# Decay rows of a gated linear attention: by transposes for the first four chunks, by earlier DMAs for the others, and a range flag summed in the tail

## The chip, the core and the metric

The kernel runs on one core of one Trainium2 chip. Its time is device microseconds (us) of one execution; the median of several runs is compared. The engines are TensorE (PE; its weight loads are shown apart as PEld), VectorE (DVE), ScalarE (ACT), GpSimd (POOL) and SyncE (SP), which here issues all DMAs. PE writes to PSUM, DVE and ACT carry results from there to SBUF.

## What is computed

A gated linear attention over 4 batches, 8 heads, 768 positions and head size 48 makes 3072 tokens of width 384. A gated product with w1, w2, w3, w_out (1024 wide) follows, then a soft mixture of 8 experts with 4 slots each, whose weights come from softmaxes of x @ phi over tokens and over slots:

```python
f = 1.0 / (1.0 + np.exp(-f_logit))
for t in range(S):
    state = f[:, :, t, :, None] * state + np.einsum('bhd,bhe->bhde', k[:, :, t], v[:, :, t])
    y[:, :, t] = np.einsum('bhd,bhde->bhe', q[:, :, t], state)
...
h = ((x @ w1) * (x @ w2)) @ w3
x = h @ w_out
...
logits = x @ phi
```

The weights w1, w2, w3 and w_out come as 64-bit floats, and the kernel decodes them on DVE.

## The kernel before, in words

The tokens are cut into 24 chunks of 128 positions; chunk n is chunk n // 4 of batch n % 4, so chunks 0 to 3 are the first ones of the four batches. In each chunk the recurrence is done as matmuls:

- `att_decay(n)` makes -log f of the forget gates on ACT and DVE (tiles in_f, nlh, nll).
- `att_scale(n)` sums it along positions with two matmuls by a triangle (pl), caps it on DVE (lc), and writes exp(-lc) into `eqp` (ACT, L561) and exp(lc) into lc. `eqp` is one tile, used again by every chunk. POOL makes kp = k * exp(lc), DVE makes qp = q * eqp (L564).
- `att_transpose(n)` transposes qp and kp in PE, four 128x128 pieces each (tq and tk), and ACT copies them out (qT, kT). The last row of eqp is what the whole chunk decays by. It is needed as columns, with the state's rows on partitions; the kernel before gets this by two DMAs (L583, L584), one from eqp into a row of DRAM (dec_d), one back as a column (dec).
- `att_scores(n)` multiplies kT by qT (pa) and DVE masks it (att, two halves). `att_out(n)` adds up the output (py) from the state and from att, takes the running minimum test okt of dec on DVE, and updates the state: pk, then tmp on DVE, then S = tmp * dec on POOL (L646).

Beside that, `w_ld`, `w_dec` and `w_low` load the six pairs of pieces of w1 and w2 (weight pairs 0 to 5), decode them in three DVE steps each (L793, L796, L799), and make the low parts of the weights (two matmuls each by identity and minus identity, pw). `glu_mm` makes the products with w1 and w2 in three passes of high and low parts (pp, L675, nine 512 column matmuls in a group). `j_ld`, `j_dec` do the same decode for w_out and w3.

The order of PE's work is written out by hand (`manual_schedule`); at the start it is att_scale(0), att_transpose(0), w_low(0), att_scores(0), w_low(1), att_out(0), att_scale(1), att_transpose(1), w_low(2), then the first GLU matmuls. The order on the other engines, and that of SP's DMAs, is chosen by a scheduler when the program is built, from when it thinks each can run. Each engine runs its own list in order, so an instruction that waits holds up all behind it.

At the very end of the chunks, `range_flag` and `range_flag2` reduce okt and the checks of the weights to one number `flag`, with one small matmul (pfl) and two DVE steps; when it is 0, a slow general version runs after. Then the tail computes the experts (`layer2`), the slots' outputs (`slot_out`) and the final sum (`combine`), and writes the output.

Of the kernel before, what the change touches and what calls it, by code (L numbers as in the profile page):

```python
# [10 lines left out]
F32 = mybir.dt.float32  # L11
# [9 lines left out]
P = 128  # L21
# [9 lines left out]
def kernel(  # L31
# [15 lines left out]
    nc = tc.nc  # L47
# [6 lines left out]
    NP = H // 2  # L54
# [3 lines left out]
    KD = DM // P  # L58
    KF = FF // P
    XB = 8  # L60
    HF = FF // 512


# [16 lines left out]
    w3_d = dpool.tile([FF, FF], F32, name="w3_d")  # L80
    wo_d = dpool.tile([FF, DM], F32, name="wo_d")
    flag = cst.tile([1, 1], I32, name="flag")
    dec_d = dpool.tile([2, H * DP], F32, name="dec_d")

    def soft_exp(pool, lg, lsum, mx):

# [466 lines left out]
    def att_scale(n):  # L553
        a = at[n]
        i = n % 2
        pl = psum.tile([P, 512], F32, tag="ps", name="pl")
        nc.tensor.matmul(pl[:, 0 : H * D], lhsT=trir, rhs=a["nlh"], start=True, stop=False)
        nc.tensor.matmul(pl[:, 0 : H * D], lhsT=trir, rhs=a["nll"], start=False, stop=True)
        lc = att_p.tile([P, H, D], F32, name="lc")
        nc.vector.tensor_scalar_min(flat(lc), pl[:, 0 : H * D], DECAY_CAP)  # L560
        nc.scalar.activation(out=eqp[:, :, 0:D], in_=lc, func=AF.Exp, scale=-1.0)  # L561
        nc.scalar.activation(out=lc, in_=lc, func=AF.Exp)  # L562
        nc.gpsimd.tensor_mul(kp[i][:, :, 0:D], a["k"], lc)  # L563
        nc.vector.tensor_mul(qp[:, :, 0:D], a["q"], eqp[:, :, 0:D])  # L564

    def att_transpose(n):
        a = at[n]
        i = n % 2
        qf = qp.rearrange("p h d -> p (h d)")
        kf = kp[i].rearrange("p h d -> p (h d)")  # L570
        tq = psum.tile([P, 512], F32, tag="ps", name="tq")
        for p in range(NP):
            nc.tensor.transpose(tq[:, p * P : (p + 1) * P], qf[:, p * P : (p + 1) * P], ident)  # L573
        qT = att_p.tile([P, NP, P], F32, name="qT")
        nc.scalar.copy(qT, tq.rearrange("p (a t) -> p a t", a=NP))
        tk = psum.tile([P, 512], F32, tag="ps", name="tk")
        for p in range(NP):
            nc.tensor.transpose(tk[:, p * P : (p + 1) * P], kf[:, p * P : (p + 1) * P], ident)  # L578
        kT = att_p.tile([P, NP, P], F32, name="kT")
        nc.scalar.copy(kT, tk.rearrange("p (a t) -> p a t", a=NP))  # L580

        dec = att_p.tile([P, NP, 1], F32, name="dec", bufs=2)
        nc.sync.dma_start(out=dec_d[n % 2 : n % 2 + 1], in_=eqp[P - 1 : P].rearrange("o h d -> o (h d)"))  # L583
        nc.sync.dma_start(out=dec.rearrange("p a o -> p (a o)"), in_=dec_d[n % 2].rearrange("(a r) -> r a", r=P))  # L584
        a.update(qT=qT, kT=kT, dec=dec, kf=kf)

    def att_scores(n):
        a = at[n]
# [407 lines left out]
    def range_flag():  # L996

        rok = keep.tile([P, 1], F32, name="rok")
        nc.vector.tensor_reduce(out=rok, in_=okt, axis=AX.X, op=ALU.min)
        cm1 = keep.tile([P, 1], F32, name="cm1")  # L1000
        for cm, lim, red, op in (
            (cmx, HI_MAX * HI_MAX, ALU.max, ALU.is_le),
            (cmn, 0.5, ALU.max, ALU.is_lt),
        ):
            nc.vector.tensor_reduce(out=cm1, in_=cm, axis=AX.X, op=red)
            nc.vector.scalar_tensor_tensor(out=rok, in0=cm1, scalar=lim, in1=rok, op0=op, op1=ALU.mult)
        return rok

    def range_flag2(rok):
        pfl = psum.tile([P, 512], F32, tag="ps", name="pfl")  # L1010
        nc.tensor.matmul(pfl[0:1, 0:1], lhsT=rok, rhs=ones, start=True, stop=True)
        okf = keep.tile([1, 1], F32, name="okf")
        nc.vector.tensor_scalar(out=okf, in0=pfl[0:1, 0:1], scalar1=P - 0.5, scalar2=None, op0=ALU.is_ge)
        nc.vector.tensor_copy(flag, okf)
# [212 lines left out]
    region.close()  # L1227
    while pf:
        pf.pop(0)()
    range_flag2(range_flag())  # L1230

    a, b, n = NCH - 3, NCH - 2, NCH - 1
    assert p == a - 1 and m_next == NCH and nchk[0] == NCK
# [42 lines left out]
    with ExitStack() as st:  # L1276
# [146 lines left out]
        def combine(t, g):  # L1423

            w = (2 - t) * P
            ot = order[used[0] % len(order)][0].tile([P, FF], F32, tag="raw", name="ot")[:, 0 : 4 * w]
            used[0] += 1
            ot = ot.rearrange("p (a f) -> p a f", a=4)
            for i in range(0, 4, 2):
                pf_ = tps.tile([P, 2, 2 * P], F32, tag="ps", name="pf")  # L1430
                for u_ in range(2):
                    nc.tensor.matmul(pf_[:, u_, :], lhsT=cT[:, 4 * g + i + u_, :], rhs=sst[t], start=True, stop=True)
                if i:
                    nc.scalar.copy(ot[:, i : i + 2], pf_[:, :, 2 * P - w : 2 * P])
                else:
                    nc.vector.tensor_copy(ot[:, i : i + 2], pf_[:, :, 2 * P - w : 2 * P])
            nc.sync.dma_start(
                out=out.rearrange("(b c p) f -> c p b f", b=B, p=P)[g, :, :, 2 * t * P : 2 * t * P + w], in_=ot
            )

        cs = range(KF)
        half = (range(KF // 2), range(KF // 2, KF))
        layer2(0, 0, cs)
# [9 lines left out]
        combine(0, 2)  # L1453
        layer2(1, 1, half[1])
        combine(0, 3)
        slot_out(1)
        combine(0, 4)
        combine(0, 5)
# [47 lines left out]
```

## Time and profile before

| | |
|---|---|
| median of 3 runs | 522.74 us (522.02 to 524.37) |
| the profiled execution | 524.82 us, of which 523.1 us are the profile's span |
| PE busy | 469.9 us (90%) |
| DVE, ACT, POOL busy | 261.4, 256.6, 95.6 us |
| mean granted TensorE clock | 0.971 of 2.4 GHz |
| moved by DMA | 85.44 MB, mean 163 GB/s |

Times in the rows are us from the span's start. A row of the timeline gives start, length, engine, line and operation, out<-in, shape, and in brackets how long the engine stood before it and what ended that. PE busy is not PE at its peak. The chain of waits is followed back from the last instruction: each piece is what released the next.

### The profile page before, as it was taken

The page shows a single profiled execution, that of the slowest core. Times are in us where ns is not written, and L with a number is a line of the kernel's source. Part 1 is how long each engine was busy: PE and PEld are TensorE (multiplying, and loading weights), DVE is VectorE, ACT ScalarE, POOL GpSimd, SP SyncE. Part 2 cuts the span into 40 slices and gives each one's busy share as a digit, 9 for nine tenths or more (in the row PEclk, how much of TensorE's full clock was granted, in tenths as well). Part 3 has the DMA queues.
Part 4 walks back from the last instruction along what each step waited for, and adds up shares of the span by engine and source line. Part 5 has one row for each costly group of instructions (what it writes and reads, how often), then busy time and mean ns, then how long its engine had stood idle before and what let it go on. Part 6 is the DMA issues. An engine that isn't in the chain of part 4 may idle for free.

```text
span 523.1 us, 12145 instructions
## 1 busy us (share of the span) xinstructions
PE 469.9 (90%) x4814; PEld 358.9 (69%) x4814; DVE 261.4 (50%) x629; ACT 256.6 (49%) x657; POOL 95.6 (18%) x124
## 2 busy tenths in 40 slices
PE   2629999999999889999999999999999999989971
PEld 1316777888887767777778777887876777734651
DVE  6736857776784455555455545453422343240131
ACT  3645566767665545455545554434477533221131
POOL 4003212311231432323232312100000010000000
PEclk9959999999999999999999999999999998999987
DMA  7993785787762744343333320019935303799977
GB/s 201 275 253 57 190 238 161 227 254 239 231 179 62 209 117 75 63 78 73 67 69 72 63 47 2 2 40 387 409 127 170 117 1 119 255 330 349 282 239 207
DMA packets 150145, 85.44 MB, mean 163 GB/s; under 512 B 115240, under 2 KB 139816, under 8 KB 149056
## 3 DMA queue, kind: packets, MB, share of 16 engines
q1 hardware_dynamic: 150080, 84.57, 56.7%
q8 instruction: 40, 0.66, 0.5%
q14 instruction: 25, 0.20, 0.1%
HBM read 74.02 MB, written 10.53 MB: 162 GB/s over the span
## 4 chain that ended last, share of the span: by engine, by line
PE 65%; DMA 9%; DVE 8%; ACT 8%; SPq 3%; issue 2%; POOL 2%; POOLq 0%; ACTq 0%; DVEq 0%
PE pp L675 32%; PE py L618 6%; DMA wck<-in_moe_w_dram 3%; ACT gT L699 2%; PE pb L1371 2%; DMA dec<-dec_d 2%; PE pb L1396 2%; PE pz L710 2%; PE pa L595 2%; PE pg L697 2%; PE pk L631 2%; PE tk L578 2%; PE tq L573 2%; SPq L529 1%; DMA raw<-in_moe_w_dram 1%
## 5 line engine op out<-in xcount | busy, mean ns | idle before, releaser
L675 PE MATMUL pp<-wt,xh 128*128 128x512 f32 x576 | 188.9, 408 | 0.6 <-ACT asb L685 0.4
L675 PEld LDWEIGHTS pp<-wt,xh 128*128 128x128 f32 x576 | 102.2, 189 | 23.6 <-issue 3.9
L675 PE MATMUL pp<-wt,xl 128*128 128x512 f32 x288 | 114.0, 396 | 0.0
L675 PEld LDWEIGHTS pp<-wt,xl 128*128 128x128 f32 x288 | 54.3, 188 | 12.3
L658 POOL TENSOR_TENSOR xl<-xT,xh 128x384 fp32r<-128x384 f32 x24 | 24.7, 1031 | 161.3 <-DVE xh L657 95.6
L685 ACT COPY asb<-pp 128x512 f32<-128x512 f32 x48 | 28.0, 583 | 44.5 <-PE pp L675 44.4
L563 POOL TENSOR_TENSOR kp<-in_k,lc 128x384 f32<-128x384 f32 x24 | 28.7, 1197 | 69.2 <-ACT lc L562 63.0
L597 DVE TENSOR_TENSOR att<-pa,tri 128x512 f32<-128x512 f32 x48 | 30.8, 679 | 11.0 <-PE pa L595 10.9
L618 PE MATMUL py<-att,vp 128*32 128x128 f32 x768 | 34.9, 273 | 1.1 <-DVE att L597 1.1
L699 ACT COPY gT<-pg 128x512 f32<-128x512 f32 x47 | 26.2, 583 | 17.2 <-PE pg L697 17.2
L646 POOL TENSOR_TENSOR S<-tmp,dec 64x192 f32<-64x192 f32 x40 | 21.6, 541 | 67.4 <-DVE tmp L642 63.8
L618 PEld LDWEIGHTS py<-att,vp 128*32 128x32 f32 x768 | 30.1, 110 | 3.7 <-DVE att L597 2.2
L561 ACT ACTIVATE eqp<-lc 128x384 f32<-128x384 f32 x24 | 12.5, 523 | 38.6 <-DVE lc L560 34.0
L573 PE MATMUL tq<-ident,qp 128*128 128x128 f32 x96 | 15.5, 286 | 17.4 <-DVE qp L564 17.3
L729 DVE TENSOR_REDUCE nbm<-pl 128x1 f32<-128x128 f32 x24 | 7.0, 291 | 46.4 <-PE pl L727 46.4
L618 PE MATMUL py<-qT,S 128*32 128x128 f32 x480 | 30.0, 273 | 0.0
L544 ACT ACTIVATE in_f<-in_f 128x384 f32<-128x384 f32 x24 | 12.6, 524 | 34.7 <-DVE in_f L543 34.7
L595 PE MATMUL pa<-qT,kT 64*128 64x128 f32 x384 | 27.9, 285 | 1.4 <-ACT kT L580 1.4
L687 DVE TENSOR_TENSOR g<-asb,pp 128x512 f32<-128x512 f32 x34 | 23.2, 684 | 11.5 <-PE pp L675 10.7
L595 PEld LDWEIGHTS pa<-qT,kT 64*128 64x128 f32 x384 | 23.3, 187 | 7.8 <-issue 4.1
L573 PEld LDWEIGHTS tq<-ident,qp 128*128 128x128 f32 x96 | 12.0, 147 | 20.0 <-issue 18.0
L550 POOL TENSOR_TENSOR nll<-in_f,nlh 128x384 fp32r<-128x384 f32 x16 | 16.3, 1017 | 36.3 <-DVE nlh L548 27.6
(173 smaller groups left out, 834.3 us busy)
## 6 DMA issues: line engine op xcount, KB each, us to landing
raw<-in_moe_w_dram SPq DMA_DIRECT2D x48, 512.0 KB
raw<-in_moe_w_dram SPq DMA_DIRECT2D x8, 1024.0 KB
wraw<-in_moe_w_dram SPq DMA_DIRECT2D x12, 512.0 KB
wck<-in_moe_w_dram SPq DMA_DIRECT2D x12, 512.0 KB
in_f<-in_f_logit_dram SPq DMA_DIRECT2D x24, 192.0 KB
in_q<-in_q_dram SPq DMA_DIRECT2D x24, 192.0 KB
in_k<-in_k_dram SPq DMA_DIRECT2D x24, 192.0 KB
vp<-in_v_dram SPq DMA_DIRECT2D x48, 96.0 KB
```

The lines of the kernel that those rows point to most:

```text
L550: (nc.vector if n < 8 else nc.gpsimd).tensor_sub(nll, nl, nlh)
L563: nc.gpsimd.tensor_mul(kp[i][:, :, 0:D], a["k"], lc)
L573: nc.tensor.transpose(tq[:, p * P : (p + 1) * P], qf[:, p * P : (p + 1) * P], ident)
L595: nc.tensor.matmul(pa[j][:, p, :], lhsT=kT[r, p, :], rhs=qT[r, p, :], start=True, stop=True)
L597: nc.vector.tensor_mul(att[:, :, j, :], pa[j], tri.rearrange("p (o t) -> p o t", o=1).to_broadcast([P, NP, P]))
L618: nc.tensor.matmul(py[y * XQ : (y + 1) * XQ, m, :], lhsT=lhsT, rhs=rhs, start=first, stop=last)
L646: nc.gpsimd.tensor_mul(st[r, :, cc], tmp[r], dec[r].to_broadcast([DP, NP, D]))
L658: nc.gpsimd.tensor_sub(xl, xT, xh)
L675: nc.tensor.matmul(pp, lhsT=xx[:, m, :], rhs=wt[hf, w, m][:, hl, :], start=(i == 0), stop=(i == 3 * KD - 1))
L685: nc.scalar.copy(s["a"], pp)
L687: nc.vector.tensor_mul(s["g"][:, cols], s["a"], pp)
L699: eng(s["gT"][:, 4 * hf : 4 * hf + 4, :].rearrange("p a t -> p (a t)"), pg)
```

## The change

- For chunks 0 to 3 (`NDT = 4`) the two DMAs of the decay row are replaced: `att_transpose` also transposes eqp in PE, four 128x128 pieces into a PSUM tile td, and DVE copies the last column of each, 128x4 in all, to dec.
- For the other chunks the two DMAs stand in `att_scale`, behind the instruction that writes eqp, rather than at the end of `att_transpose`. dec has three buffers instead of two, and dec_d four rows.
- `range_flag2` moves from ahead of the last three chunks' GLU into the tail, between `combine(0, 3)` and `slot_out(1)`, with its PSUM tile from the tail's pool; `range_flag`, its DVE part, moves to the head of that part of the tail in the code.

```diff
--- before.py
+++ after.py
@@ -58,6 +58,7 @@
     KD = DM // P
     KF = FF // P
     XB = 8
+    NDT = 4
     HF = FF // 512
 
 
@@ -80,7 +81,7 @@
     w3_d = dpool.tile([FF, FF], F32, name="w3_d")
     wo_d = dpool.tile([FF, DM], F32, name="wo_d")
     flag = cst.tile([1, 1], I32, name="flag")
-    dec_d = dpool.tile([2, H * DP], F32, name="dec_d")
+    dec_d = dpool.tile([4, H * DP], F32, name="dec_d")
 
     def soft_exp(pool, lg, lsum, mx):
 
@@ -559,6 +560,11 @@
         lc = att_p.tile([P, H, D], F32, name="lc")
         nc.vector.tensor_scalar_min(flat(lc), pl[:, 0 : H * D], DECAY_CAP)
         nc.scalar.activation(out=eqp[:, :, 0:D], in_=lc, func=AF.Exp, scale=-1.0)
+
+        a["dec"] = dec = att_p.tile([P, NP, 1], F32, name="dec", bufs=3)
+        if n >= NDT:
+            nc.sync.dma_start(out=dec_d[n % 4 : n % 4 + 1], in_=eqp[P - 1 : P].rearrange("o h d -> o (h d)"))
+            nc.sync.dma_start(out=dec.rearrange("p a o -> p (a o)"), in_=dec_d[n % 4].rearrange("(a r) -> r a", r=P))
         nc.scalar.activation(out=lc, in_=lc, func=AF.Exp)
         nc.gpsimd.tensor_mul(kp[i][:, :, 0:D], a["k"], lc)
         nc.vector.tensor_mul(qp[:, :, 0:D], a["q"], eqp[:, :, 0:D])
@@ -578,11 +584,13 @@
             nc.tensor.transpose(tk[:, p * P : (p + 1) * P], kf[:, p * P : (p + 1) * P], ident)
         kT = att_p.tile([P, NP, P], F32, name="kT")
         nc.scalar.copy(kT, tk.rearrange("p (a t) -> p a t", a=NP))
-
-        dec = att_p.tile([P, NP, 1], F32, name="dec", bufs=2)
-        nc.sync.dma_start(out=dec_d[n % 2 : n % 2 + 1], in_=eqp[P - 1 : P].rearrange("o h d -> o (h d)"))
-        nc.sync.dma_start(out=dec.rearrange("p a o -> p (a o)"), in_=dec_d[n % 2].rearrange("(a r) -> r a", r=P))
-        a.update(qT=qT, kT=kT, dec=dec, kf=kf)
+        if n < NDT:
+            ef = eqp.rearrange("p h d -> p (h d)")
+            td = psum.tile([P, 512], F32, tag="ps", name="td")
+            for p in range(NP):
+                nc.tensor.transpose(td[:, p * P : (p + 1) * P], ef[:, p * P : (p + 1) * P], ident)
+            nc.vector.tensor_copy(a["dec"], td.rearrange("p (a t) -> p a t", a=NP)[:, :, P - 1 : P])
+        a.update(qT=qT, kT=kT, kf=kf)
 
     def att_scores(n):
         a = at[n]
@@ -1006,8 +1014,8 @@
             nc.vector.scalar_tensor_tensor(out=rok, in0=cm1, scalar=lim, in1=rok, op0=op, op1=ALU.mult)
         return rok
 
-    def range_flag2(rok):
-        pfl = psum.tile([P, 512], F32, tag="ps", name="pfl")
+    def range_flag2(rok, tps):
+        pfl = tps.tile([P, 512], F32, tag="ps", name="pfl")
         nc.tensor.matmul(pfl[0:1, 0:1], lhsT=rok, rhs=ones, start=True, stop=True)
         okf = keep.tile([1, 1], F32, name="okf")
         nc.vector.tensor_scalar(out=okf, in0=pfl[0:1, 0:1], scalar1=P - 0.5, scalar2=None, op0=ALU.is_ge)
@@ -1227,7 +1235,6 @@
     region.close()
     while pf:
         pf.pop(0)()
-    range_flag2(range_flag())
 
     a, b, n = NCH - 3, NCH - 2, NCH - 1
     assert p == a - 1 and m_next == NCH and nchk[0] == NCK
@@ -1438,6 +1445,7 @@
                 out=out.rearrange("(b c p) f -> c p b f", b=B, p=P)[g, :, :, 2 * t * P : 2 * t * P + w], in_=ot
             )
 
+        rok = range_flag()
         cs = range(KF)
         half = (range(KF // 2), range(KF // 2, KF))
         layer2(0, 0, cs)
@@ -1453,6 +1461,7 @@
         combine(0, 2)
         layer2(1, 1, half[1])
         combine(0, 3)
+        range_flag2(rok, tps)
         slot_out(1)
         combine(0, 4)
         combine(0, 5)
```

What the scheduler makes of it is seen at three places. In the rows a number behind a name is the buffer's own.

On SP, behind the loads of weight pair 5, before:

```order
L1061 DMA pht_214<-in_moe2_phi_dram 128x3x32
L583 DMA dec_d_78<-eqp_123 1x512
L512 DMA in_f_208<-in_f_logit_dram 128x8x48
L529 DMA vp0_131<-in_v_dram 128x4x48 x2
L512 DMA in_f_216<-in_f_logit_dram 128x8x48
L584 DMA dec_258<-dec_d_78 128x4x1
L583 DMA dec_d_78<-eqp_123 1x512
L512 DMA in_q_210<-in_q_dram 128x8x48
L512 DMA in_k_212<-in_k_dram 128x8x48
L584 DMA dec_372<-dec_d_78 128x4x1
```

The changed kernel:

```order
L1069 DMA pht_214<-in_moe2_phi_dram 128x3x32
L513 DMA in_f_208<-in_f_logit_dram 128x8x48
L530 DMA vp0_131<-in_v_dram 128x4x48 x2
L513 DMA in_q_210<-in_q_dram 128x8x48
L513 DMA in_k_212<-in_k_dram 128x8x48
L513 DMA in_f_216<-in_f_logit_dram 128x8x48
L513 DMA in_q_218<-in_q_dram 128x8x48
L530 DMA vp1_132<-in_v_dram 128x4x48
L513 DMA in_k_220<-in_k_dram 128x8x48
```

The four DMAs of chunks 0 and 1 are gone, and q, k of chunk 3 (in_q_210, in_k_212) stand ahead of f of chunk 4 (in_f_216).

On DVE, from the mask product of chunk 0 (att_275, att_279 in the change) to chunk 1's qp (qp<-in_q_185) before; the row ahead of the first one shown is the product's first half:

```order
L597 TENSOR_TENSOR att_275<-pa_277,tri_137 128x4x128
L796 SCALAR_TENSOR_TENSOR wf_303<-wraw_182,wf_303 128x1024
L550 TENSOR_TENSOR nll_301<-in_f_180,nlh_299 128x384
L799 SCALAR_TENSOR_TENSOR wf_303<-wraw_182,wf_303 128x1024
L642 TENSOR_TENSOR tmp_338<-pk_329,S0_142 64x192 x2
L560 TENSOR_SCALAR lc_352<-pl_349 128x384
L793 TENSOR_SCALAR wf_436<-wraw_191 128x1024
L796 SCALAR_TENSOR_TENSOR wf_436<-wraw_191,wf_436 128x1024
L543 TENSOR_SCALAR in_f_194<-in_f_194 128x384
L799 SCALAR_TENSOR_TENSOR wf_436<-wraw_191,wf_436 128x1024
L550 TENSOR_TENSOR nll_401<-in_f_194,nlh_399 128x384
L564 TENSOR_TENSOR qp_124<-in_q_185,eqp_123 128x8x48
```

The changed kernel, from that first half on:

```order
L605 TENSOR_TENSOR att_279<-pa_280,tri_137 128x4x128
L804 SCALAR_TENSOR_TENSOR wf_307<-wraw_182,wf_307 128x1024
L605 TENSOR_TENSOR att_279<-pa_281,tri_137 128x4x128
L551 TENSOR_TENSOR nll_305<-in_f_180,nlh_303 128x384
L807 SCALAR_TENSOR_TENSOR wf_307<-wraw_182,wf_307 128x1024
L650 TENSOR_TENSOR tmp_342<-pk_333,S0_142 64x192 x2
L561 TENSOR_SCALAR lc_356<-pl_353 128x384
L801 TENSOR_SCALAR wf_445<-wraw_191 128x1024
L570 TENSOR_TENSOR qp_124<-in_q_185,eqp_123 128x8x48
L804 SCALAR_TENSOR_TENSOR wf_445<-wraw_191,wf_445 128x1024
L544 TENSOR_SCALAR in_f_194<-in_f_194 128x384
L807 SCALAR_TENSOR_TENSOR wf_445<-wraw_191,wf_445 128x1024
```

The product's second half stands behind one decode step of weight pair 2 (wf_307); qp of chunk 1 stands ahead of two steps of pair 3 (wf_445) and no longer behind nll of chunk 2 and all three of them.

On SP much later, from chunk 10's write of eqp's row to the first loads of w3 (w3raw), before:

```order
L583 DMA dec_d_78<-eqp_123 1x512
L512 DMA in_q_1984<-in_q_dram 128x8x48
L512 DMA in_k_1986<-in_k_dram 128x8x48
L529 DMA vp0_131<-in_v_dram 128x4x48 x2
L584 DMA dec_2091<-dec_d_78 128x4x1
L1137 DMA w3raw_2417<-w3_d_75 128x1024
```

The changed kernel:

```order
L566 DMA dec_d_78<-eqp_123 1x512
L513 DMA in_q_2003<-in_q_dram 128x8x48
L513 DMA in_k_2005<-in_k_dram 128x8x48
L530 DMA vp0_131<-in_v_dram 128x4x48
L567 DMA dec_1988<-dec_d_78 128x4x1
L530 DMA vp0_131<-in_v_dram 128x4x48
L1145 DMA w3raw_2436<-w3_d_75 128x1024
```

The write stands where it stood; the load of dec has moved ahead of one of the two v loads.

## Rows read from the trace of the kernel before

**Rows 1.** The page: its first line, and PE's busy tenths in 40 equal slices.

```profile
span 523.1 us, 12145 instructions
...
PE   2629999999999889999999999999999999989971
```

**Rows 2.** Waits, 0 to 60 us: who waited for whom, us in total, times, longest us.

```profile
PE tq L573 <- DVE qp L564: 17.3, 2, 13.2
...
ACT eqp L561 <- DMA dec_d<-eqp: 4.6, 1, 4.6
```

**Rows 3.** Timeline, 22 to 43 us: start us, us, engine line op, [idle before <-releaser].

```profile
22.60 0.33 PE L558 MATMUL pl<-nll,trir 128*128 128x384 f32 x1
...
23.70 0.56 DVE L560 TENSOR_SCALAR lc<-pl 128x384 f32<-128x384 f32 x1
...
27.17 0.35 DVE L543 TENSOR_SCALAR in_f<-in_f 128x384 f32<-128x384 f32 x1
...
28.99 0.37 SPq L583 DMA_DIRECT2D dec_d<-eqp  x1
...
34.82 0.52 ACT L561 ACTIVATE eqp<-lc 128x384 f32<-128x384 f32 x1 [4.58 <-DMA dec_d<-eqp]
...
35.38 0.56 DVE L564 TENSOR_TENSOR qp<-in_q,eqp 128x384 f32<-128x384 f32 x1 [5.07 <-ACT eqp L561]
...
36.08 1.08 PE L573 MATMUL tq<-ident,qp 128*128 128x128 f32 x4 [13.15 <-DVE qp L564]
...
41.83 0.16 DVE L619 SCALAR_TENSOR_TENSOR okt<-dec,okt 128x4 f32<-128x4 f32 x1 [2.71 <-DMA dec<-dec_d]
...
42.04 0.63 PE L675 MATMUL pp<-wt,xh 128*128 128x512 f32 x2
```

**Rows 4.** Busy by windows of 2 us: engines' us (instructions), granted clock (PEclk), DMA share, GB/s.

```profile
24.00:26.00 2.00, 0.00 (x0) 0.00 (x0) 0.95 (x2) 0.21 (x1) 0.00 (x0) 0.67 1.06 226
...
40.00:42.00 2.00, 2.00 (x4) 0.90 (x4) 0.16 (x1) 0.89 (x2) 0.14 (x1) 0.56 0.29 31
```

**Rows 5.** Timeline, 12 to 26 us: PE, DVE and two loads that SP issues.

```profile
12.18 1.06 PE L578 MATMUL tk<-ident,kp 128*128 128x128 f32 x4
12.29 2.50 SPq L512 DMA_DIRECT2D in_k<-in_k_dram  x1
...
18.36 1.10 PE L853 MATMUL pw<-wf,ident 128*128 128x512 f32 x2 [1.03 <-DVE wf L799]
...
19.02 1.28 DVE L597 TENSOR_TENSOR att<-pa,tri 128x512 f32<-128x512 f32 x2
...
19.67 0.38 SPq L512 DMA_DIRECT2D in_f<-in_f_logit_dram  x1
...
20.22 1.21 DVE L796 SCALAR_TENSOR_TENSOR wf<-wraw,wf 128x1024 uint32<-128x1024 uint32 x1
...
25.29 0.69 DVE L793 TENSOR_SCALAR wf<-wraw 128x1024 uint32<-128x1024 uint32 x1 [1.04 <-DMA wraw<-in_moe_w_dram]
```

**Rows 6.** Timeline of PE, 46 to 92 us.

```profile
47.94 1.08 PE L618 MATMUL py<-att,vp 128*32 128x128 f32 x32
...
49.55 0.66 PE L573 MATMUL tq<-ident,qp 128*128 128x128 f32 x4
...
89.76 0.30 PE L618 MATMUL py<-att,vp 128*32 128x128 f32 x2 [1.05 <-DVE att L597]
```

**Rows 7.** SP's timeline and the chain, 158 to 205 us: start us, us, what.

```profile
174.38 1.32 SPq L529 DMA_DIRECT2D vp<-in_v_dram  x2
...
175.80 2.69 DMA dec<-dec_d
...
185.84 3.63 DMA dec<-dec_d
```

**Rows 8.** Chain, 425 to 440 us: start us, us, what.

```profile
432.88 0.06 DVE flag L1014
```

**Rows 9.** Chain, 495 us to the end.

```profile
512.23 0.37 ACT ot L1434
```

## The prediction, made before the result was known

> **What bounds the kernel now.** Read the page's slices first, 13.1 us each: TensorE (PE) is busy nine tenths or more in nearly all of them, but in the first three it shows 2, 6 and 2 tenths [rows 1]. The third, 26 to 39 us, is no longer the start, so the question is what holds PE there. The waits of the first 60 us, longest first, name one: PE stood 13.2 us at one step, the q transposes (tq, two waits of 17.3 us in all), for DVE's qp, and ACT stood 4.6 us at eqp for the transfer out of eqp (dec_d<-eqp) [rows 2]. The timeline shows the chain in order [rows 3]. Chunk 1's prefix sums leave PE at 22.93 (22.60 + 0.33). DVE has capped them (lc) at 24.26. Then ACT should write eqp, but chunk 0's last row of eqp has still to be copied out by a DMA, which SP issues at 28.99 behind the weight loads, and eqp is written at 34.82 only. qp follows at 35.38, and tq starts at 36.08 after 13.15 us of idle. While PE stood, its granted clock fell (0.67 on average in 24 to 26 us, that is from 2.4 to 1.2 GHz) and was 0.56 on average even in 40 to 42 us [rows 4]. So the eight transposes and four long matmuls of the weights' low parts that follow ran to 42.04 before the first GLU matmul could start [rows 3].
>
> **The change, part by part.**
>
> *The DMA out of eqp goes, for chunks 0 to 3.* What eqp(1) then waits for is lc(1) alone. Going by the rows that are there, lc ends at 24.26, eqp takes 0.52, qp 0.56 [rows 3]: tq could start at 25.4. But DVE's order has changed too. The second half of chunk 0's mask product (two together 1.28) now stands behind one 1.21 us decode step [rows 5], and chunk 0's output matmuls, the running state and lc(1) all come after it, so lc(1) ends about 1.2 later, at 25.5. Ahead of qp(1) now stands a decode step of 0.69 whose weights are there by 25.29 [rows 5]: 25.5 to 26.2. eqp is written beside it. qp ends at 26.8, tq starts at about 26.9 instead of 36.08. **Gain 9.2**, at most 10.7.
>
> *The transposes come in, four a chunk, for chunks 0 to 3.* Chunk 0's (price: tk's, 1.06 [rows 5]) push the low parts of weight pair 0 and the scores back by that, but 1 us later PE stands 1.03 for a decode [rows 5], which takes it up: 0. That cover gone, it would be 1.06. Chunk 1's stand in the stretch at 1.2 GHz, at tq's price of 1.08 [rows 3]; those of chunks 2 and 3 cost 0.66 each, as tq did at 49.55 [rows 6]. **Cost 1.08 + 2 x 0.66 = 2.4.** PE is the pace there, so nothing hides it.
>
> *DVE's copy of the decay row* (128x4, from PSUM) isn't in the trace. The nearest row is okt on the same 128x4 shape, 0.16 [rows 3]; I take that, and at the most 0.56, what lc's cap of 384 columns out of PSUM takes [rows 3]. It takes the place of waits: okt stood 2.71 for its DMA at 41.83 [rows 3]. Behind the copy on DVE stand nll(2), the decode of weight pair 4 and the mask products of chunk 1; by the sum above its transposes end at about 26.9 + 3 x 1.08 = 30.1, and the products are wanted 9 us later, so 0. Later PE stands 1.05 for a mask product at 89.76 [rows 6], while DVE has been let off more than PE: 0 to 1.05 comes back, I take 0.5.
>
> *The later chunks' DMAs.* In the rows of SP's order they stand where they stood: the scheduler had placed them as soon as eqp was written. One dec load moves ahead of one v load, where two v loads took 1.32 to issue, and that dec transfer (2.69) was on the chain [rows 7]. The half of 1.32 bounds the gain; I take 0.2. The further slots of dec and dec_d end no wait that the trace shows: 0, with 6.3 as the most (both transfers of [rows 7], 2.69 + 3.63).
>
> *The flag.* Its matmul and two small DVE steps leave a stretch in which one of the two shows on the chain for 0.06 [rows 8]: with the other 0.1 gained. In the tail they stand between output copies. ACT's last copy ends at 512.60 [rows 9], 10.5 us before the span of 523.1 [rows 1] does; output transfers fill that, and if its three steps all delayed the last output, at okt's 0.16 each, it would be 0.5. I take 0.
>
> **Sum**: 9.2 - 2.4 + 0.5 + 0.2 + 0.1 = 7.6 us less. The profiled execution took 524.82, which gives 517.2; it stands 2.08 above the median of the runs, so the median goes from 522.74 to **515.1**. The clock is taken as before: PE restarts at 1.2 GHz in both, and gets 2.4 back some 5.7 us later (0.56 in 40 to 42 puts the rise at 41.76 [rows 4]). Bounds of the terms: the wait 9.2 to 10.7, the transposes 2.0 to 3.5, the rest 0 to 1.3. That makes 5.7 to 10.0 less at the outside, some 513.5 to 516.5 where the middle of them holds. Later waits are relative to PE, and shift with it.
>
> **Rivals.**
>
> *The clock doesn't fall* (512.4). PE would stand some 2.7 us (1.2 later than 22.93, to 26.9) in place of 13.15. From 36.08 to 42.04 it ran 5.96; tq took 1.08 cold and 0.66 warm, so warm the stretch would be some 3.6, and the new transposes 0.66: 2.4 + 0.4 less, near 2.7. For it: the stand shrinks to a fifth. Against it: the clock fell within some 2 us of PE's stop at 22.93 (mean 0.67 in 24 to 26) [rows 3, 4], and 2.7 is longer than that. The Trainium skill says in "Perfetto Trace Analysis", section Matmul Optimizations, that the matmul engine scales its power with its use, so that matmuls should run back to back in batches. The fall after 22.93 agrees with it. By that rule, filling most of the stand would bring the clock back as well, and the sum would be 10.3 instead of 7.6; it doesn't tell how short the stand has to be, so the row decides, and the case has a small chance.
>
> *The weights are late* (516.7 to 519.7). DVE decodes weight pair 4 at 42.01 now; it would ask for it at about 33. The transfers were issued before 28.99, and the DMA engines are full (share 1.06 in 24 to 26) and are drained only in 40 to 42 (0.29) [rows 4]. Chunk 1's mask product stands behind that decode (0.69 + 1.21 + 1.21, then 1.28), and PE's output matmuls want it at about 39.8 (the first GLU matmul at 33.9, plus the 5.9 from 42.04 to 47.94 in the trace [rows 3, 6]). Weights that land at 37 cost 1.6, at 40 4.6. Against it: in_f of chunk 2, issued at 19.67 into the same backlog, was used at 27.17 [rows 3, 5]; 7.5 us from 28.99 at the latest give 36.5, a cost of 1.1 at most.
>
> *The stand remains, slower* (525.3 to 527.0). If in_k of chunk 1, issued at 12.29, were not there before the engines drain, tk(1) would start no sooner than now, whatever eqp does, and sixteen transposes would be pure cost: 4 x 0.66 to 4 x 1.08. It decides if in_k lands after about 36. Against it: in_f of chunk 2, issued later, at 19.67, was read by DVE at 27.17 [rows 3, 5]. The Trainium skill, "DMA: Bandwidth & Descriptors", section Queues, rings and completion order, says that transfers of one issuing engine need not complete in the order of their issue; taken strictly it makes that evidence worthless. The trace gives in_k no landing of its own, so the case keeps a chance.
>
> *The later DMAs do gain* (down to 509), if the further slots end waits that the order doesn't show. Chain rows allow 6.3 at most [rows 7]; nothing in SP's order speaks for it.
>
> **How the numbers follow.** A measurement of this kernel can tell 0.5%, 2.6 us, from no change: 520.1 and 525.4 are the marks. The forecast (513.5 to 516.5) has 0.66, the clock that stays up 0.12, the late weights 0.12, the stand that remains 0.05, gains from later DMAs 0.05. Faster by over 0.5%: all but the last tail of the late weights and the stand, 0.92; slower 0.04; the same 0.04. The range goes from the second case less some spread, 511.5, to within the late weights, 519.0; what lies outside is the stand, the far ends of the late weights and of the later DMAs.
>
> **What would show it.** Right: ACT's wait for dec_d<-eqp is gone; tq(1) starts at 26 to 28 with 2 to 4 us of idle before it; the first GLU matmul at about 34; td groups of 1.1 once and 0.66 after; the third slice of PE's row well above 2; chunk 4 onward and the tail as before, some 7 us earlier. Wrong: tq or tk of chunk 1 after 30 with a DMA as releaser; DVE's decode of pair 4 waiting for wraw, with PE at py waiting for att after 40; a shift that is 7 us at 45 us and much smaller at 100.

## The result, and the profile after

| | before | changed |
|---|---|---|
| median, first comparison | 522.98 us (522.02 to 524.37, 4 runs) | 516.99 us (514.53 to 519.87, 4 runs) |
| ratio, 95% interval | | 0.9886 [0.9851, 0.9922] |
| median, second comparison | 521.44 us (519.13 to 523.18, 15 runs) | 514.97 us (514.02 to 517.59, 6 runs) |
| ratio, 95% interval | | 0.9886 [0.9857, 0.9914] |
| the profiled execution, and its span | 524.82, 523.1 us | 514.53, 512.8 us |

The change is worth 1.1%: 6.0 us by the first medians, 6.5 by the second. Forecast were 7.6 less and 515.1. The two profiled executions differ by 10.3 us, more than the medians do; where the some 4 us between come from is told below.

The page of the changed kernel, first line, PE's slices and the granted clock:

```profile
span 512.8 us, 12160 instructions
...
PE   2789999999999879999999999999999998989981
...
PEclk9989999999999989999999999999999999989997
```

The second and third slices went from 6 and 2 [rows 1] to 7 and 8 tenths. The waits of the first 60 us:

```profile
PE tq L579 <- DVE qp L570: 6.8, 2, 4.0
...
ACT eqp L562 <- DVE lc L561: 4.0, 3, 2.4
```

The longest wait at tq fell from 13.2 [rows 2] to 4.0 us, and ACT's wait at eqp for a DMA is gone; what it waits for now is lc (DVE's capped sums). The timeline, 12 to 42 us:

```profile
12.34 1.06 PE L591 MATMUL td<-ident,eqp 128*128 128x128 f32 x4
...
13.44 0.16 DVE L592 COPY dec<-td 128x4 f32<-128x4 f32 x1 [1.03 <-PE td L591]
...
22.91 0.34 PE L559 MATMUL pl<-nll,trir 128*128 128x384 f32 x1
...
23.54 0.56 DVE L561 TENSOR_SCALAR lc<-pl 128x384 f32<-128x384 f32 x1
...
24.14 0.52 ACT L562 ACTIVATE eqp<-lc 128x384 f32<-128x384 f32 x1
...
25.03 0.95 DVE L801 TENSOR_SCALAR wf<-wraw 128x1024 uint32<-128x1024 uint32 x1 [0.92 <-DMA wraw<-in_moe_w_dram]
25.38 1.44 POOL L569 TENSOR_TENSOR kp<-in_k,lc 128x384 f32<-128x384 f32 x1
25.89 1.34 DVE L570 TENSOR_TENSOR qp<-in_q,eqp 128x384 f32<-128x384 f32 x1
...
27.30 0.96 PE L579 MATMUL tq<-ident,qp 128*128 128x128 f32 x4 [4.05 <-DVE qp L570]
...
28.05 1.06 PE L584 MATMUL tk<-ident,kp 128*128 128x128 f32 x4
...
28.90 1.06 PE L591 MATMUL td<-ident,eqp 128*128 128x128 f32 x4
...
32.49 0.69 DVE L801 TENSOR_SCALAR wf<-wraw 128x1024 uint32<-128x1024 uint32 x1 [0.64 <-PE pw L861]
...
32.52 0.63 PE L683 MATMUL pp<-wt,xh 128*128 128x512 f32 x2
...
38.41 1.08 PE L626 MATMUL py<-att,vp 128*32 128x128 f32 x32
...
40.95 0.60 PE L591 MATMUL td<-ident,eqp 128*128 128x128 f32 x4
```

Read it against [rows 3]: eqp of chunk 1 is written at 24.14 instead of 34.82, tq starts at 27.30 instead of 36.08, and the first GLU matmul (pp) at 32.52 instead of 42.04, 9.5 us earlier. DVE's decode of weight pair 4 (the L801 at 32.49) waits for PE and not for its weights, and py of chunk 1 at 38.41 waits for nothing worth a bracket.

The clock, in windows of 2 us as in [rows 4]:

```profile
26.00:28.00 2.00, 0.70 (x4) 0.71 (x5) 2.00 (x2) 0.00 (x0) 0.82 (x1) 0.88 0.95 181
28.00:30.00 2.00, 2.00 (x11) 2.00 (x10) 1.78 (x3) 1.68 (x4) 0.00 (x0) 0.50 0.98 304
30.00:32.00 2.00, 2.00 (x6) 0.95 (x5) 0.88 (x3) 2.00 (x5) 0.00 (x0) 0.77 1.02 404
```

0.88 on average is 0.48 us at 1.2 GHz in that window, 0.77 is 0.92 us: the clock fell at 27.5, 0.2 us after PE had begun again, and was back at 30.9. That is 3.4 us at half clock. Before it was 17.1: from 24.7 (0.67 in 24 to 26) to 41.76 [rows 4]. A second execution of the changed kernel (first experiment) differs here:

```profile
26.00:28.00 2.00, 0.57 (x3) 0.57 (x4) 2.00 (x3) 0.00 (x0) 0.36 (x1) 0.50 0.97 185
...
32.00:34.00 2.00, 2.00 (x6) 1.18 (x6) 0.59 (x2) 0.88 (x3) 0.00 (x0) 0.80 1.00 382
```

It stood at half clock from 26.0 to 32.8, 6.8 us. Of the eleven profiles in which chunk 1's eqp no longer waits, five show 3.4 us there and six 6.8.

**How the gain runs through the program.** The copies asb<-pp on ACT come twice for each chunk of the GLU; their starts in the timeline are milestones. Shift against the kernel before, in us (minus is earlier); the names are those of the experiments:

| kernel | 1st copy | 15th | 17th | 37th | end of span |
|---|---|---|---|---|---|
| before, start | 44.31 | 176.80 | 201.00 | 385.93 | 523.1 |
| changed | -9.53 | -9.99 | -7.16 | -7.19 | -10.3 |
| changed, second profile | -8.48 | -7.84 | -7.05 | -7.02 | -10.1 |
| transposes only | -9.20 | -9.98 | -9.49 | -9.45 | -11.1 |
| early DMAs only | -1.02 | +0.55 | +1.72 | +1.72 | -1.7 |
| two eqp tiles | -7.84 | -9.38 | -8.52 | -8.81 | -11.6 |
| changed, flag left | -8.61 | -5.70 | -4.46 | -4.50 | -6.2 |
| transposes and further slots | -7.56 | -6.92 | -5.82 | -5.75 | -10.8 |
| flag only | -0.28 | -0.57 | -0.53 | -0.57 | -4.2 |
| chunk 0's transposes only | -9.23 | -9.03 | -9.13 | -9.37 | -12.4 |
| the same, second profile | -8.75 | -8.58 | -8.82 | -9.07 | -12.2 |
| changed, block apart | -9.45 | -5.85 | -7.79 | -7.56 | -11.6 |
| chunk 0's transposes only, block apart | -8.85 | -8.83 | -10.05 | -8.49 | -10.3 |
| transposes only, block apart | -8.33 | -8.56 | -9.48 | -8.78 | -11.9 |

The rows behind the 15th and the 17th copy, before:

```profile
176.80 0.57 ACT L685 COPY asb<-pp 128x512 f32<-128x512 f32 x1
...
201.00 0.59 ACT L685 COPY asb<-pp 128x512 f32<-128x512 f32 x1 [1.64 <-PE pp L675]
```

and in the changed kernel:

```profile
166.81 0.57 ACT L693 COPY asb<-pp 128x512 f32<-128x512 f32 x1
...
193.84 0.59 ACT L693 COPY asb<-pp 128x512 f32<-128x512 f32 x1 [2.76 <-PE pp L683]
```

Every kernel, also those whose tail is that of the kernel before (early DMAs only, two eqp tiles), reaches the end 1.6 to 5.1 us better than it stood at the 37th copy. So the profiled execution of before lost some 3 us behind 386 us that most others don't lose. Its page shows a fall of the clock there, the 8 of the 34th slice, 431.6 to 444.6 us (3.4 us at half clock, so some 1.7 of the 3):

```profile
PEclk9959999999999999999999999999999998999987
```

The 10.3 us between the two profiles are 7 us of change and 3 us of that execution. The column to go by is the 37th copy: there the changed kernel stands 7.2 and 7.0 us ahead, near the 6.0 and 6.5 of the medians and the 7.6 of the sum.

### The profile page after: what moved, and what is told of

It is laid out like the page before. It is cut to its first block, busy times and chain, and to the rows that moved or that the text cites. A ratio compares the mean times of both kernels' runs of the same rounds, so it can differ in the third digit from the quotient of the medians.

```text
span 512.8 us, 12160 instructions
## 1 busy us (share of the span) xinstructions
PE 470.1 (92%) x4830; PEld 360.6 (70%) x4830; DVE 262.6 (51%) x633; ACT 256.5 (50%) x657; POOL 96.2 (19%) x124
## 4 chain that ended last, share of the span: by engine, by line
PE 66%; ACT 9%; DVE 8%; DMA 8%; issue 3%; SPq 3%; POOL 1%; ACTq 0%; DVEq 0%; POOLq 0%
PE pp L683 32%; PE py L626 7%; ACT gT L707 3%; DMA wck<-in_moe_w_dram 2%; PE pk L639 2%; PE pb L1378 2%; PE pz L718 2%; PE tq L579 2%; PE pb L1403 2%; PE tk L584 2%; PE pg L705 2%; PE pa L603 2%; DMA in_f<-in_f_logit_dram 2%; DMA raw<-in_moe_w_dram 1%; SPq L530 1%
## 5 line engine op out<-in xcount | busy, mean ns | idle before, releaser
L683 PEld LDWEIGHTS pp<-wt,xl 128*128 128x128 f32 x288 | 54.1, 188 | 12.2
L626 PE MATMUL py<-att,vp 128*32 128x128 f32 x768 | 36.7, 279 | 1.4 <-DVE att L605 1.3
L605 DVE TENSOR_TENSOR att<-pa,tri 128x512 f32<-128x512 f32 x48 | 30.9, 679 | 10.9 <-PE pa L603 10.9
L626 PEld LDWEIGHTS py<-att,vp 128*32 128x32 f32 x768 | 31.2, 112 | 4.1 <-DVE att L605 2.2
L626 PE MATMUL py<-qT,S 128*32 128x128 f32 x480 | 30.9, 278 | 0.0
L603 PEld LDWEIGHTS pa<-qT,kT 64*128 64x128 f32 x384 | 23.3, 187 | 7.3 <-issue 3.8
L626 PEld LDWEIGHTS py<-qT,S 128*32 128x32 f32 x480 | 23.2, 112 | 0.0
L718 PE MATMUL pz<-gT,wps 128*32 128x128 f32 x384 | 17.9, 279 | 4.9 <-ACT gT L707 3.9
```

The source lines that it names most:

```text
L603: nc.tensor.matmul(pa[j][:, p, :], lhsT=kT[r, p, :], rhs=qT[r, p, :], start=True, stop=True)
L605: nc.vector.tensor_mul(att[:, :, j, :], pa[j], tri.rearrange("p (o t) -> p o t", o=1).to_broadcast([P, NP, P]))
L626: nc.tensor.matmul(py[y * XQ : (y + 1) * XQ, m, :], lhsT=lhsT, rhs=rhs, start=first, stop=last)
L683: nc.tensor.matmul(pp, lhsT=xx[:, m, :], rhs=wt[hf, w, m][:, hl, :], start=(i == 0), stop=(i == 3 * KD - 1))
L718: nc.tensor.matmul(pz[q_ * NS : (q_ + 1) * NS, 0:P], lhsT=wps[:, m, :], rhs=s["gT"][:, m, :], start=(i == 0), stop=(i == KF // NQ - 1),)
```

## The experiments

Each comparison has its own runs of the kernel before, with medians of 521.33 to 522.11 us from here on. Experiments 1 to 4 ran on one chip, 5 to 8 on a second, 9 and 10 on a third, 11 on a fourth; across these groups the ratios are the better comparison. "Block" is the five loads of w3raw (rows of the next layer's weights) that stand together on SP, before at 176 us, in the changed kernel at 167:

```profile
176.31 2.69 SPq L1137 DMA_DIRECT2D w3raw<-w_d  x5
...
167.02 2.63 SPq L1145 DMA_DIRECT2D w3raw<-w_d  x5
```

**1. The changed kernel again**, unchanged, for the spread and a second profile.

> The changed kernel once more, for a second profile beside the first one (512.8 us) and for its spread: its four runs lay between 514.5 and 519.9 us. Theory (the wait for eqp is what went): 0.985 to 0.993 of the kernel before, with the first wt-stage GLU matmul at 32 to 34 us again whatever the total is, so that what differs between a fast and a slow run lies later. Rival (the start itself varies): in a slow run the first GLU matmul comes 3 to 5 us later.

Measured: 514.97 us (514.02 to 517.59), ratio 0.9886 [0.9857, 0.9914]. In this second profile the clock stayed at half until 32.8 and the first pp started at 33.58, 1 us later than in the first. The gain stands; by the 17th copy the two profiles are level, so that 1 us at the start doesn't reach the end.

**2. The transposes alone**: DMAs of chunks 4 on, slots and flag as before.

```diff
         dec = att_p.tile([P, NP, 1], F32, name="dec", bufs=2)
+        if n < NDT:
+            ...
+            nc.vector.tensor_copy(dec, td.rearrange("p (a t) -> p a t", a=NP)[:, :, P - 1 : P])
+        else:
+            nc.sync.dma_start(out=dec_d[n % 2 : n % 2 + 1], ...
```

> Only the transposes of chunks 0 to 3; the later chunks' DMAs, their two slots and the flag stay as before. Theory (the freed eqp is all of it): the same as the changed kernel within 0.3%, chunk 1's tq at 26 to 28 us. Rival 1 (the later DMAs or their further slots carry part): 2 to 6 us slower than the changed kernel. Rival 2 (the flag's place carries part): 1 to 2 us slower than the changed kernel, from about 430 us on.

Measured: 513.47 us (510.99 to 514.22), ratio 0.9839 [0.9811, 0.9867]. The whole gain is here. The median is 1.5 us below that of the changed kernel, but the intervals of the two ratios overlap.

**3. The early DMAs alone**, for all chunks (NDT = 0), with the further slots; no transposes, flag as before.

```diff
-    NDT = 4
+    NDT = 0
...
+    range_flag2(range_flag())
...
-        rok = range_flag()
...
-        range_flag2(rok, tps)
```

> Only the DMAs: in all 24 chunks they stand behind the instruction that writes eqp, with three slots of dec and four rows of dec_d; no transposes, the flag as before. Theory: the scheduler leaves chunk 0's DMA behind the weight loads on SP, so eqp is written at about 35 us as before and the time is that of the kernel before, 0.997 to 1.003. Rival (beginning the DMAs earlier and more slots gain by themselves): 0.985 to 0.995.

Measured: 523.23 us (522.57 to 529.26, 10 runs), ratio 1.006 [1.0031, 1.0089]: slower. Its timeline has the stand of before, unchanged:

```profile
34.77 0.52 ACT L562 ACTIVATE eqp<-lc 128x384 f32<-128x384 f32 x1 [4.70 <-DMA dec_d<-eqp]
...
36.03 1.08 PE L579 MATMUL tq<-ident,qp 128*128 128x128 f32 x4 [13.71 <-DVE qp L570]
```

and its chain, 175 to 201 us, shows where 1.2 us went between the 15th and the 17th copy:

```profile
180.71 6.62 DMA in_f<-in_f_logit_dram
...
196.67 2.85 PE py L626 x56
199.52 0.88 PE pk L639 x16
```

An in_f load (gates of a later chunk) issued behind the block took 6.62 us, and py and pk, 1.53 and 0.60 elsewhere on the chain, then ran at the lower clock (half from 196.7 to 200.1), which cost 1.6 us. That is one execution. More than this stage, 1.4 us, was lost between the 1st and the 3rd copy (43.29 to 69.92 us, where the kernel before takes 44.31 to 69.52), beside chunks that the changed kernel serves with transposes. So this experiment doesn't give the price of the later chunks' DMAs alone.

**4. Two tiles of eqp**, used in turn by chunks 0 to 2, all DMAs where they were, no transposes.

```diff
+    eqps = [wr.tile([P, H, DP], F32, tag="eqp0", name="eqp0", bufs=1), eqp]
+    nc.vector.memset(eqps[0], 1.0)
...
+        eqp = eqps[n % 2 if n < 3 else 1]
         nc.scalar.activation(out=eqp[:, :, 0:D], in_=lc, func=AF.Exp, scale=-1.0)
```

> The kernel before with all its DMAs, but chunks 0 and 2 write a tile of their own in place of eqp, so chunk 1 needn't wait for chunk 0's DMA; no transposes. Theory (the wait for the one eqp buffer cost the time): chunk 1's tq at 25 to 28 us, and 8 to 10 us less than before at the first GLU matmul, as no transposes are paid; in the end 0.980 to 0.992, if okt on DVE, still waiting for the DMA of chunk 0 in front of weight pair 4, doesn't give some of it back (then 0.990 to 0.998). Rival (PE would stand there anyway, for loads): tq at 33 us or later, 0.997 to 1.005.

Measured: 515.34 us (513.18 to 515.66), ratio 0.9881 [0.9855, 0.9906], the changed kernel's gain without a transpose. Its timeline:

```profile
24.44 0.52 ACT L562 ACTIVATE eqp<-lc 128x384 f32<-128x384 f32 x1
...
28.07 0.34 SPq L585 DMA_DIRECT2D dec_d<-eqp  x1
...
28.68 1.12 PE L574 MATMUL tq<-ident,qp 128*128 128x128 f32 x4 [5.10 <-DVE qp L565]
...
34.23 0.63 PE L677 MATMUL pp<-wt,xh 128*128 128x512 f32 x2
```

The transfer out of chunk 0's eqp is as late as before (issued at 28.07), but eqp of chunk 1 is written at 24.44. So what cost the time was the one buffer of eqp, not the way in which the decay row travels.

**5. The changed kernel with the flag left where it was.**

```diff
+    range_flag2(range_flag())
...
-        rok = range_flag()
...
-        range_flag2(rok, tps)
```

> The changed kernel with the range flag left where it was before: transposes for chunks 0 to 3 and the later chunks' DMAs at their new place, with the further slots. It is the kernel with the transposes alone plus the new DMA place and slots. Theory L (what the later DMAs' part takes back is real): the time of the changed kernel within 0.3% (514 to 517 us), some 1 to 2 us above the kernel with the transposes alone. Rival F (it is the moved flag that takes it back): the time of the kernel with the transposes alone, 512.5 to 514 us, and the stretch of clock 0.5 in the last layer's start, at 454 us in the changed kernel, is gone.

Measured: 516.73 us (511.18 to 519.63; 516.59 without the longest run, which the ratio leaves out), ratio 0.9869 [0.983, 0.9908]. By the median theory L, but the other five runs spread over 7.4 us, so alone it tells little. The stretch of half clock at 454 us was gone here, and came at 428 and 496 us.

**6. The further slots alone**, beside the transposes, with the DMAs in their old place.

```diff
-    dec_d = dpool.tile([2, H * DP], F32, name="dec_d")
+    dec_d = dpool.tile([4, H * DP], F32, name="dec_d")
...
-        dec = att_p.tile([P, NP, 1], F32, name="dec", bufs=2)
+        dec = att_p.tile([P, NP, 1], F32, name="dec", bufs=3)
```

> The transposes for chunks 0 to 3, the later chunks' DMAs in their old place, but with three buffers of dec and four rows of dec_d. Every engine's order is that of the kernel with the transposes alone; only the waits for free slots differ. Theory L with the slots as cause: 514 to 517 us. L with the place as cause, and F: 513.5 within 0.3%, as the kernel with the transposes alone. If a slot ended a wait there would be a gain: under 512.

Measured: 515.22 us (513.82 to 517.59), ratio 0.9883 [0.9857, 0.9909]. No gain from slots, as forecast. The median lies in the range of theory L with the slots as cause, 1.75 us above the second experiment, but that ran on another chip and the intervals of the ratios overlap: whether the slots cost anything is open.

**7. The flag's move alone.**

```diff
-    range_flag2(range_flag())
...
+        rok = range_flag()
...
+        range_flag2(rok, tps)
```

> The kernel before with the flag's three steps moved into the tail and nothing else. The prediction's term: 0.1 us less, so no difference that can be told (ratio 0.998 to 1.002). Rival F: slower by 1 to 3 us, with PE's clock at half for some us behind 460 us, where the flag's matmul is gone from the order.

Measured: 520.94 us (519.12 to 523.56, 12 runs), ratio 0.9992 [0.9971, 1.0012]. No difference; rival F falls.

**8. Transposes for chunk 0 alone** (the second experiment with NDT = 1), with a second profile.

> Transposes for chunk 0 alone; chunks 1 to 3 use the two DMAs again, the flag and the later DMAs stand as before. Theory T (the time was the wait of eqp of chunk 1 for the transfer out of chunk 0's eqp): tq of chunk 1 starts at 27 to 28 us as with all four, and the twelve further transposes (1.06 + 2 x 0.60 us) are saved as far as the transfers of chunks 1 to 3 come in time: 511.0 to 513.5 us. Rival B (the same wait moves on to chunk 2, whose eqp then waits for chunk 1's transfer behind the weight loads): ACT's eqp of chunk 2 or the running state of chunk 1 waits for a DMA at 38 to 42 us, with 514 to 517 us.

> A second look at the kernel with chunk 0's transposes alone, on the same chip as the two with the block of loads taken apart. As before: tq of chunk 1 at 27 to 28 us, 512 to 516 us.

Measured: 514.4 us (512.47 to 517.11), ratio 0.9872 [0.9848, 0.9897]; the second execution took 512.56. The first one's timeline:

```profile
27.09 1.11 PE L574 MATMUL tq<-ident,qp 128*128 128x128 f32 x4 [4.04 <-DVE qp L565]
...
32.79 0.63 PE L683 MATMUL pp<-wt,xh 128*128 128x512 f32 x2
...
34.73 0.36 SPq L591 DMA_DIRECT2D dec_d<-eqp  x1
...
38.64 0.51 ACT L562 ACTIVATE eqp<-lc 128x384 f32<-128x384 f32 x1
```

tq starts as early as with all four. Chunk 1's transfer, issued at 34.73, leaves eqp of chunk 2 unhindered at 38.64 (in the changed kernel it is written at 37.66), and the running state of chunk 1 (S on POOL, at 42.36) waits for no DMA, so the wait of rival B isn't there. Yet the time lies in B's range, and above theory T's 511.0 to 513.5: the twelve transposes saved bring nothing that can be told.

**9. The changed kernel with the block taken apart.** One load is asked for in each step of the GLU (two chunks of the attention), and held back by one element that ACT copies out of eqp in that step.

```diff
         w3s.append(pool.tile([P, FF], F32, tag="raw", name="w3raw"))
+        if c < K0:
+            nc.scalar.copy(w3s[-1][0:1, 0:1], eqp[0:1, 0, 0:1])
...
     def prefetch():
-        for _ in range(2):
+        npre[0] += 1
+        if pf and len(w3s) < K0 and npre[0] % 4:
+            return
+        for _ in range(1 if len(w3s) < K0 else 2):
```

> The changed kernel, with the first five loads of the next layer's weight rows (w3raw, 512 KB each), which now stand as one block at 167 us, taken apart: one every two chunks, each held back by a one-element copy on ACT out of eqp, so that it lands among the chunks' own loads from about 190 to 300 us. Theory W (what the changed kernel loses against its start is lost where that block crowds out the chunk loads and decay rows at 165 to 195 us): no wait for in_f or dec over 3.5 us there, the shift against the kernel before stays near 9 us from the first GLU matmul to 385 us instead of falling to 7.2, and the time is 510 to 513 us. Rival N (the loss there is of another kind, the clock or the order): the shift still falls by over 1.5 us between 167 and 194 us, and the time stays at 514 to 517 us.

Measured: 513.46 us (512.88 to 514.43), ratio 0.9863 [0.9833, 0.9893]; all five runs are within 1.6 us, where those of the changed kernel spread over 5.3 (four runs) and 3.6 (six). The intervals of the two ratios overlap, so a gain in time isn't shown. The chain of the changed kernel, 165 to 195 us, with the block issued at 167.02:

```profile
166.04 2.68 DMA dec<-dec_d
...
172.97 1.53 PE py L626 x56
...
187.81 2.75 PE py L626 x56
190.56 0.97 PE pk L639 x16
```

and with the block apart there is no DMA on it, and no slow py:

```profile
176.19 1.53 PE py L626 x56
...
188.75 1.53 PE py L626 x56
190.28 0.60 PE pk L639 x16
```

Busy time of that stage, 170 to 180 us (PE, PEld, DVE, ACT, POOL, clock, DMA share, GB/s), of the changed kernel:

```profile
170.00:180.00 10.00, 8.65 (x124) 7.20 (x122) 3.00 (x7) 4.34 (x10) 3.28 (x4) 1.00 0.98 286
```

and with the block apart:

```profile
170.00:180.00 10.00, 9.24 (x131) 7.36 (x130) 5.08 (x11) 6.33 (x15) 3.01 (x4) 1.00 0.51 91
```

Between the 15th and the 17th copy this kernel gains 1.9 us on the kernel before, where the changed one loses 2.8 and, in its second profile, 0.8. Theory W holds for that place, but not for the time, which lies just above its range, nor for the shift: this execution had fallen from 9.5 to 5.9 us ahead by the 15th copy.

The shift hides that the kernel before pays at its block too. In all eleven profiles with the block the stretch from the 15th to the 17th copy takes 24.0 to 27.0 us (24.2 before), in the three with it apart 22.3 to 23.3. From the 17th to the 37th, where the five loads then lie, it is the other way round: 184.6 to 185.0 us with the block, 185.2 to 186.5 with it apart.

**10. Chunk 0's transposes alone, block apart.**

> Transposes for chunk 0 alone, the later chunks' DMAs, slots and flag as before, and the block of five w3raw loads taken apart as in the other kernel. Theory W: the stall at 165 to 195 us goes here too, where the kernel with the block lost little against before but both stood some 4 to 7 us for transfers; 508 to 512 us, the best of all. Rival N: 512.5 to 515.5 us, as with the block.

Measured: 513.82 us (511.97 to 515.23), ratio 0.9862 [0.9831, 0.9892]: rival N. With the block this kernel lost nothing there against the kernel before (-9.03 to -9.13). Taken apart, it gains 1.2 us there (-8.83 to -10.05), and loses 1.6 until the 37th copy (-8.49); that the moved loads are what costs it there was not tested.

**11. All four chunks' transposes, block apart**, later DMAs, slots and flag as before.

> Transposes for chunks 0 to 3, the later chunks' DMAs, slots and flag as before, and the block of five w3raw loads taken apart. It differs from the changed kernel with the block apart (513.46 us) by the later DMAs' place, the slots and the flag alone, and is the best candidate by the runs so far. Theory L (the new place of the later DMAs costs by itself): 510.5 to 512.5 us, 1 to 3 us below that kernel. Rival (what they cost was their meeting with the block, or run-to-run spread): 513.5 us within 1, no difference.

Measured: 513.17 us (512.24 to 513.69), ratio 0.9831 [0.9786, 0.9876]. Against the ninth experiment the new place of the DMAs, the slots and the flag make 0.3 us by the medians, and theory L's 510.5 to 512.5 isn't met. By the ratios, each to the kernel before on its own chip, it is 0.3%, some 1.7 us, with overlapping intervals: L is not supported, but a cost of 1 to 2 us isn't ruled out. This is the lowest median of several runs, and each of its six is below the lowest of the changed kernel's ten (514.02), which ran on other chips.

## Why the prediction was right, point by point

**The place and the cause: right.** The wait of eqp's one buffer for chunk 0's transfer was the time. The fourth experiment shows it without transposes, the eighth with one chunk's, and the third that without either the stand remains.

**tq of chunk 1 at 26.9: came at 27.30, gain 8.8 instead of 9.2.** Two sizes were off and nearly cancel. lc was there at 24.10 and not at 25.5: the decode step that now stands between the two halves of the mask product, with chunk 0's transposes, put the last pl back by 0.31 us (22.91 instead of 22.60 [rows 3]), not by 1.2. In turn the next decode (L801) waited 0.92 for its weights, and qp took 1.34 instead of 0.56, beside POOL's kp. The stand before tq came out at 4.05 us, where the prediction had 2.7.

**The transposes: right in price, less in cost.** 1.06 for chunks 0 and 1, 0.60 for chunk 2 (0.66 forecast), and the DVE copy 0.16 as taken from okt. The sets of chunks 2 and 3 lie between the 1st and the 3rd copy; that stretch took 25.21 us before (44.31 to 69.52) and 25.29 after (34.78 to 60.07). So of 1.2 us 0.1 is left (0.3 in the second profile, 35.83 to 61.33), more given back than the 0.5 of the sum; "nothing hides it" was wrong. Chunk 0's 1.06 were taken up, as forecast, but for a part of those 0.31. That twelve fewer transposes change nothing (eighth experiment) agrees.

**The clock "taken as before": this step was mis-sized.** PE did not work 5.7 us at 1.2 GHz from its new start, but 3.4, and 5.4 in the second profile (27.43 to 32.8). So the first GLU matmul came at 32.52 and 33.58 where the sum had 33.9. The rival in which the clock doesn't fall is ruled out: it fell in all eleven profiles with the shorter stand. The Trainium skill's advice in "Perfetto Trace Analysis", section Matmul Optimizations, to run matmuls back to back because the engine scales its power with its use, agrees with both kernels; the 17.1 us before and 3.4 or 6.8 after are this case's.

**"Later waits are relative to PE, and shift with it": true only in part.** The block did shift, from 176.31 to 167.02, and the kernel before has its waits there as well (dec of 2.69 and 3.63 us [rows 7]). But the kernel stood 10.0 us ahead at the 15th copy (7.8 in the second profile; the sum had 7.3 there) and 7.2 (7.1) at the 17th. Of the 2.8 us, 1.6 are py and pk at the lower clock (half from 187.9 to 191.4), which the second profile doesn't have there. In that profile an in_f load behind the block took 7.86 us. How the rest comes about isn't settled. The other kernels with the block and the freed eqp lie between a gain of 0.2 and a loss of 1.2 at this place; with the block apart the loss is gone.

**The sum, 7.6 against 6.0 and 6.5: in part luck.** A start that was 0.3 to 1.4 better than the sum had it and a loss of 0.8 to 2.8 at the block that it did not have nearly cancel; so it came close to the 7.0 to 7.2 at the 37th copy. The second median, 514.97, lies in the forecast's 513.5 to 516.5. The first, 516.99, lies above it, where the prediction had put the late weights; they were not late.

**The later DMAs, 0.2 gained, "0 to 6.3": no gain, and what they cost is open.** For all chunks, without transposes, they made the kernel 0.6% slower (third experiment); of the 2.7 us that its profile lost between the 1st and the 37th copy, 1.4 went beside chunks that the changed kernel serves with transposes. The second and the eleventh experiment, without the DMAs' new place, the slots and the flag's move, have lower ratios than the first and the ninth, with overlapping intervals. The lower bound of 0 in the prediction had no row behind it. The long wait for in_f behind the block isn't peculiar to their new place: with the DMAs in the old one the second experiment's chain has it too.

```profile
171.73 6.06 DMA in_f<-in_f_logit_dram
```

**The flag, 0.1 gained: nothing that can be told**, 0.9992 [0.9971, 1.0012].

**The other rivals.** Late weights: ruled out; the decode of pair 4 waits for PE, and py of chunk 1 started at 38.41. The stand that remains: ruled out, tk ran at 28.05. That case rested on the rule of the Trainium skill in "DMA: Bandwidth & Descriptors", section Queues, rings and completion order, that transfers of one issuer need not end in order; no run here shows in_k late, and none refutes the rule.

**What stays open.** Runs of one kernel differ by 1.5 us (eleventh experiment) to 7 us (fifth). Profiles show single falls of the clock at varying places (188 and 454 us in the changed kernel, 423 in the second experiment, 428 in the fifth), and the stretch from the 1st to the 15th copy takes 131.0 to 136.1 us; what decides between them wasn't settled. That the changed kernel is worse than the second or eleventh experiment by 0.3% rests on medians with overlapping intervals.

## What to carry to other kernels

When a slow transfer holds up an engine, ask first whether someone waits for its data or only for the buffer that it reads: a second buffer alone gave 6.1 us here, the sixteen transposes alone 8.0. A block of loads far behind the change moves along with the work and can cost the kernel before as much, so read such a stage in its own length, and not only as a shift between two kernels. And a profile differs from the median of its kernel: compare milestones of several kernels before a stage that the change doesn't touch is given a meaning.

## What the runs showed that was not expected

- DVE and POOL slowed each other. qp took 1.34 us and kp 1.44 where they lay side by side (25.38 to 27.23), against 0.56 for qp [rows 3] and 1.12 for kp in the kernel with two eqp tiles, where qp ran later (0.55) and a decode step beside kp took 2.01 instead of 1.21. Here qp ended 0.41 us after kp did (26.82). The Trainium skill says in "SBUF — State Buffer", section SBUF: two separate sides, that a DVE instruction with two SBUF inputs and a GpSimd instruction that reads SBUF take a shared port pair by turns, and that the one that comes second is blocked for the whole instruction; that qp, begun second, ended after kp agrees, that kp took longer too is not explained by it.
- The granted clock fell at 27.5 us, when PE had already been working for 0.2 us and its stand of 4.05 us was over. In the second execution of the same kernel it fell at 26.0, 2.7 us into the stand, and before 1.8 us into it (24.7, after PE's stop at 22.93 [rows 3]). What sets the moment isn't shown.
- Five loads of 512 KB, wanted by PE only from 453.90 us on, lengthen the stretch beside them to 24.0 to 27.0 us from 22.3 to 23.3. Taken apart they give part of that back later, and no change of the median can be told. The runs of the three kernels with them apart spread over 1.5 to 3.3 us, those of kernels with the block over 2.5 and more; whether the block makes the spread isn't shown.
